# Far stretches of the attention visits in another order, and mixing weights loaded in quarters

## The chip, the cores and the metric

The kernel runs on one core of a Trainium2 chip. Its metric is the device time of one execution in microseconds, as the median of several runs. The engines are TensorE (PE, with its weight loads shown apart as PEld), VectorE (DVE), ScalarE (ACT), GpSimd (POOL) and SyncE (SP), which here only issues transfers.

## What is computed

The result is the sum of the input and two branches, which both read the same normalised input (2048 tokens of 512 features, bf16):

```python
xn = _layernorm(x)
return x + _A_ref(xn, A_wqkv, A_wo) + _B_ref(xn, B_w_in, B_w_sp, B_b_sp, B_w_out)

# A: attention, 32 heads of 16 features, sliding causal band of 256 keys
scores = einsum('bhqd,bhkd->bhqk', q, k) * Dh ** -0.5
mask = (idx[:, None] - idx[None, :] >= 0) & (idx[:, None] - idx[None, :] < 256)
p = softmax(where(mask, scores, -1e9)); o = einsum('bhqk,bhkd->bhqd', p, v)
A = o.reshape(B, S, D) @ wo

# B: gated unit that mixes along the tokens with a full 2048 x 2048 matrix
z = gelu(xn @ w_in); z1 = z[..., :688]; z2 = _layernorm(z[..., 688:])
g = einsum('ts,bsf->btf', w_sp, z2) + b_sp[None, :, None]
B = (z1 * g) @ w_out
```

## The kernel before

The 2048 tokens are 16 blocks of 128. The order of all work is written out by hand, as three strings of tokens (STAGE1, STAGE2, STAGE3). A token is a letter with arguments, and a table names the function that each letter calls; every engine gets its instructions in the order in which the tokens emit them. No planner moves anything, and each engine's queue is worked through in order.

Stage 1 loads and normalises the input (`a`, `A`, `b`), transposes it to feature-major `xnT` (by a DMA transpose on SP, token `d`, line 301, for 13 of the blocks; one such transpose is 128 x 512), and computes the gates: matmuls at line 311 (`z`), GELU on ACT (`y`). Its last tokens already project keys and queries (line 341), which are spread over the partitions by DMAs (`G` for keys, line 389; `F` for queries, line 368). For the first head group the spreads are issued on SP, for the others on POOL.

Stage 2 is the attention, in four groups of 8 heads, with the mixing and all projections woven between. For one head group the band of scores is laid out along one axis: key block kb owns 320 columns, the queries that its 128 keys can reach in two halves (its keys 64 to 127 are stored against queries shifted by 64, so that both half-blocks of keys share one layout). `S` computes 512 columns of scores for 4 heads (line 431, 8 to 16 matmuls in 32-row tiles), `X` takes the exponential on ACT (line 445), `M` multiplies the edges with a mask on DVE.

A **visit** (`V`, function `visit`, matmuls at line 512) multiplies these exponentials with the values. Unit u of a group is 256 queries. Visit i does two things at once: the *near* half of unit i, which reads keys 0 to 63 of each key block on partitions 0 to 63, and the *far* half of unit i - 1, which reads keys 64 to 127 on partitions 64 to 127. The two halves lie in different rows of the TensorE array and write different PSUM banks (`oP`), so they stream side by side. `av_half` lists a half's *stretches*: a stretch is one key block and one e (which four of the eight heads), n columns wide, and consists of four pairs of weight load and matmul, one for each of four heads, in four column strips of the array (64 rows x 17 columns of weights each). A half has up to eight stretches of 64, 128, 192 or 256 columns, 1280 columns in all for each strip; with u = 0 it has four of them, 768 columns near and 512 far. `av_half` yields each stretch with the column `at` which it begins, counted along its half, and `visit` sorts the stretches of both halves by that column, near before far where they are equal. This gives the order of the matmuls on TensorE. Before the change the far half runs from wide to narrow (256, 256, 192, 192, 128, 128, 64, 64), and the near half from narrow to wide, apart from that with u = 1, which runs from wide to narrow. There are 33 visits, i = 0 to 32, the last with a far half alone.

`N` normalises a finished unit on DVE. `H` is the mixing (line 553): 16 matmuls of 344 columns for each half of a block n. Its weights are a transposed 128 x 2048 slice of the mixing matrix, a tile of `wsp_pool`, which has three buffers. `load_wsp` (token `w`, line 545) fetches it with DMA transposes on SP, part 0 and part 1 in two tokens that stand next to each other. `w` of block n + 3 stands shortly behind the last mixing of block n, whose buffer it takes, and so it waits on SP until TensorE has read that buffer. `u` (line 566) transposes the gated result `z1u` of one block, also on SP. `O` and `R` are the output projections (lines 583 and 589), `v` stores a block of the result: blocks 0 to 2 on POOL, the others on SP (line 632). Stage 3 ends the projections.

SP therefore serves, in this order: input loads; transposes of x, with the weights of mixing block 0 (`w,0,0 w,0,1`) between the eighth and the ninth; the spreads of the first head group, with the weights of blocks 1 and 2 between them; then mixing weights and transposes of z1u in turn; at the end the stores.

Of the kernel before, what the change touches and what calls it, by code (L numbers as in the profile page):

```python
# [8 lines left out]
P = 128  # L9
# [12 lines left out]
NB = S_TOK // P  # L22
# [9 lines left out]
BAND = 320  # L32
WARM = 29
NCEN = 3


def kb_start(kb):
    return BAND * kb if kb < NB - 1 else BAND * (NB - 2) + 256


def kb_len(kb):
    return min(BAND, S_TOK - kb * P)
# [135 lines left out]
def kernel(  # L178
# [12 lines left out]
    nc = tc.nc  # L191
# [56 lines left out]
    xs = s1.tile([P, NB, D], BF, name="xs")  # L248
    xc = s1.tile([P, NCEN, D], BF, name="xc")
    xcT = s1.tile([P, NCEN, NDC, P], BF, name="xcT")  # L250

# [30 lines left out]
    def x_transpose(n, bank):  # L282
        xn = xc[:, n, :] if n < NCEN else xs[:, n, :]
        tp = banks[bank].bitcast(BF)[:, 0:512].rearrange("p (c q) -> p c q", c=NDC)
        for c in range(NDC):
            nc.tensor.transpose(out=tp[:, c, :], in_=xn[:, c * P : (c + 1) * P], identity=ident[:])  # L286

    def x_copy(n, bank, eng):
        tp = banks[bank].bitcast(BF)[:, 0:512].rearrange("p (c q) -> p c q", c=NDC)
        if n < NCEN:  # L290
            for c in (0, 2):
# [14 lines left out]
    def gate(n, half, tag, p0, p1):  # L306
        zp = zrot[tag]
        f0 = half * FH
        for c in range(2 * p0, 2 * p1):
            for lo, hi in Z_RANGES:  # L310
                nc.tensor.matmul(  # L311
                    zp[:, lo:hi],
                    lhsT=xcT[:, n, c, :] if n < NCEN else xnT[:, c, n * P : (n + 1) * P],
                    rhs=w_in_sb[:, c, f0 + lo : f0 + hi],
# [4 lines left out]
    def gelu(n, half, tag):  # L319
        zp = zrot[tag]  # L320
        dst = z1u[:, n + 1, 0:FH] if half == 0 else z2[:, n, :]

        scale = rstdx[:, n : n + 1] if n < NCEN else 1.0
        nc.scalar.activation(out=dst, in_=zp[:, 0:FH], func=ACT.Gelu_apprx_tanh, scale=scale)  # L324
# [142 lines left out]
    def av_half(G, u, half):  # L467

        a = 2 * u
        r0 = 64 * half
        bank = oP[(G * 8 + u) % 2]
        todo = []
        for kb in range(max(0, a - 2), a + 2):

            lo = max(0, a * P - kb * P - r0)
            hi = min(kb_len(kb) - (r0 if kb >= NB - 2 else 0), (a + 2) * P - kb * P - r0)
            assert lo < hi, (u, half, kb)
            todo += [(hi - lo, kb, lo, hi, e) for e in range(2)]  # L480

        up = half == 0 and (G * 8 + u) % 8 != 1
        todo.sort(key=lambda t: (t[0] if up else -t[0], t[1], t[4]))
        at = 0
        for i, (n, kb, lo, hi, e) in enumerate(todo):
            o0 = e * 256 + kb * P + lo + r0 - a * P
            col = (kb_start(kb) + lo) % RING
            yield at, [
                dict(
                    out=bank[32 * s : 32 * s + DH + 1, o0 : o0 + n],  # L490
                    lhsT=v_all[r0 : r0 + 64, kb, HG * G + 4 * e + s, :],
                    rhs=E[r0 : r0 + 64, 4 * e + s, col : col + n],
                    start=(half == 0 and i == 0),
                    stop=(half == 1 and i == len(todo) - 1),
                )
                for s in range(4)
            ]
            at += n

    def visit(i):  # L500

        top = list(av_half(i // 8, i % 8, 0)) if i < NG * 8 else []
        low = list(av_half((i - 1) // 8, (i - 1) % 8, 1)) if i >= 1 else []
        if not top:

            nc.tensor.matmul(
                oP[i % 2][0 : DH + 1, 0:1], lhsT=v_all[0:64, 0, 0, :], rhs=E[0:64, 0, 0:1],
                start=True, stop=True, skip_group_check=True,
            )
        for _, four in sorted(top + low, key=lambda t: t[0]):  # L510
            for args in four:
                nc.tensor.matmul(skip_group_check=True, **args)  # L512
# [26 lines left out]
    wsp_tiles = {}  # L539

    def load_wsp(n, part):
        if part == 0:
            wsp_tiles[n] = wsp_pool.tile([P, NB, P], BF, name="wspT")
        c0 = part * NB // 2
        nc.sync.dma_start_transpose(
            out=wsp_tiles[n][:, c0 : c0 + NB // 2, :],
            in_=B_w_sp[n * P : (n + 1) * P, c0 * P : (c0 + NB // 2) * P],
        )

    def mix(n, half, bank, c0, c1):  # L550
        w = wsp_tiles[n]
# [82 lines left out]
    def set_o():  # L634
# [7 lines left out]
        "Q": proj_q, "q": keep_q, "K": proj_k, "k": keep_k, "F": spread_q, "G": spread_k, "P": proj_v, "p": keep_v,  # L642
        "H": mix, "h": keep_mix, "u": transpose_u, "O": out_u, "R": out_o, "o": keep_out, "v": store_out,
        "w": load_wsp, "f": out_u_half, "g": out_o_half, "x": store_half, "r": load_xres, "m": set_o,
    }

# [68 lines left out]
    for r0 in (0, 64):  # L715
        nc.gpsimd.affine_select(
            out=mask[r0 : r0 + 64, 0, :], in_=mask[r0 : r0 + 64, 0, :], pattern=[[-1, 64]],
# [3 lines left out]
            out=mask[r0 : r0 + 64, 1, :], in_=mask[r0 : r0 + 64, 1, :], pattern=[[1, 64]],  # L721
# [54 lines left out]
```

## Time and profile before

| | |
|---|---|
| median of 3 runs | 258.38 us (258.15 to 258.97) |
| profiled execution, its own time | 258.61 us |
| its span, first to last instruction | 256.9 us |
| PE busy | 248.8 us (97%) |
| DVE busy | 186.2 us (72%) |
| ACT busy | 181.0 us (70%) |
| POOL busy | 92.0 us (36%) |
| granted TensorE clock | 1.000 |

A group row of the profile reads: line, engine, operation, written tile <- read tiles, rows * columns of the array, shapes, count | busy us, mean ns of one | idle us ahead of it, and what ended the idle time. A row of the timeline reads: start, duration, engine, line, operation, tiles, shape of the first of the merged instructions, count. SPq is SyncE's queue at work issuing a DMA; the time is that of the issue, not of the transfer. A row that names a line with three numbers (1232/1304/4387) gives the least, the median and the longest duration in ns. In the windows view a row is a stretch of time, its length, and for each engine the busy time and in brackets the number of instructions that touch it. The ends of matmuls are modelled by the profiler, so that a visit's length is read from the start of its first matmul to the start of the next work.

### The profile page before, as it was taken

What the parts mean: (1) busy time and instruction counts of PE and PEld (TensorE: products, weight loads), DVE (VectorE), ACT (ScalarE), POOL (GpSimd) and SP (SyncE); (2) the same over time, 40 slices, a digit from 0 to 9 for tenths busy, and PEclk for the clock granted to TensorE, in tenths of its full rate; (3) what the DMA queues carried; (4) which work ended last, traced back from release to release, by engine and by line L of the source; (5) the groups of instructions that cost most, each with busy time, mean ns of one, the idle gap of its engine ahead of it and who ended that gap; (6) DMA issues with size and microseconds to landing.
All of it is one profiled execution on the core that took longest, in us unless ns stands there. A gap on an engine that the chain in (4) does not pass through costs nothing.

```text
span 256.9 us, 9051 instructions
## 1 busy us (share of the span) xinstructions
PE 248.8 (97%) x3900; PEld 139.3 (54%) x3936; DVE 186.2 (72%) x412; ACT 181.0 (70%) x142; POOL 92.0 (36%) x172
## 2 busy tenths in 40 slices
PE   7999999999999999999999999999999999999995
PEld 6565555433456555655555655655555544444454
DVE  4887877888797676768775767758877487666764
ACT  3686566899978687777778776867687787777400
POOL 7514110430016176017288053603645343611110
PEclk9999999999999999999999999999999999999999
DMA  7985743269404886659969549998775632644432
GB/s 233 362 242 103 124 82 81 72 134 220 100 3 86 111 148 137 116 110 133 145 125 166 115 83 113 128 148 146 140 144 114 125 74 84 115 123 119 115 98 68
DMA packets 69945, 32.67 MB, mean 127 GB/s; under 512 B 60833, under 2 KB 66945, under 8 KB 69905
## 3 DMA queue, kind: packets, MB, share of 16 engines
q1 hardware_dynamic: 64000, 20.79, 44.1%
q0 software_dynamic: 4672, 9.97, 17.6%
q10 hardware_dynamic: 1232, 1.32, 1.5%
q8 instruction: 31, 0.51, 0.9%
q14 instruction: 10, 0.07, 0.1%
HBM read 8.41 MB, written 2.10 MB: 41 GB/s over the span
## 4 chain that ended last, share of the span: by engine, by line
PE 93%; ACT 3%; issue 1%; DMA 1%; DVE 1%
PE w L553 31%; PE sS L431 10%; PE w L341 10%; PE oP L512 8%; PE w L583 6%; PE zb L311 5%; PE za L311 5%; PE zo L311 5%; PE w L396 4%; PE w L589 4%; ACT E L445 2%; DMA xs<-in_A_x_dram 1%; PE w L286 1%; PE w L605 1%; PE tj L583 1%
## 5 line engine op out<-in xcount | busy, mean ns | idle before, releaser
L445 ACT ACTIVATE E<-sS 128x2048 bf16<-128x2048 f32 x76 | 142.6, 1877 | 41.9 <-PE sS L431 40.8
L553 PE MATMUL w<-z,wspT 128*128 128x344 bf16 x512 | 92.6, 310 | 0.7 <-issue 0.2
L553 PEld LDWEIGHTS <-wspT 128*128 128x128 bf16 x512 | 46.9, 98 | 31.5 <-issue 5.9
L389 POOL DMA_DIRECT2D kbd<-kz x48 | 29.5, 623 | 60.4 <-DVE kz L381 58.3
L368 POOL DMA_DIRECT2D q<-qs x54 | 28.0, 529 | 29.2 <-DVE qs L357 22.0
L454 DVE TENSOR_TENSOR E<-E,mask 128x1024 bf16<-128x1024 bf16 x52 | 34.7, 675 | 4.3 <-ACT E L445 4.3
L341 PE MATMUL w<-xnT,wqkv 128*128 128x512 bf16 x106 | 35.7, 380 | 0.7 <-issue 0.3
L431 PE MATMUL sS<-q,kbd 32*128 32x320 bf16 (+4 forms) x816 | 30.4, 244 | 0.3
L560 DVE SCALAR_TENSOR_TENSOR z1u<-w,b_all,z1u 128x344 bf16<-128x344 f32 x32 | 18.2, 568 | 16.4 <-PE w L553 16.3
L520 DVE STREAM_TRANSPOSE a<-oP 128x512 f32<-128x512 f32 x32 | 22.7, 709 | 5.4 <-PE oP L512 5.3
L512 PE MATMUL oP<-E,v_all 64*17 64x256 bf16 (+3 forms) x1920 | 24.8, 230 | 0.4 <-issue 0.4
L512 PEld LDWEIGHTS <-v_all 64*17 64x17 bf16 x1920 | 20.2, 85 | 9.0 <-issue 8.8
L311 PEld LDWEIGHTS <-xnT 128*128 128x128 bf16 x208 | 18.3, 98 | 12.4
L431 PEld LDWEIGHTS <-kbd 32*128 32x128 bf16 x816 | 12.2, 92 | 22.2 <-issue 20.0
L583 PE MATMUL w<-w_out_sb,z1u 128*128 128x512 bf16 x67 | 19.1, 380 | 0.5 <-issue 0.3
L577 POOL DMA_DIRECT2D wqkv<-in_A_x_dram x16 | 8.9, 558 | 28.3 <-DVE out_sb L597 27.5
L341 PEld LDWEIGHTS <-wqkv 128*128 128x128 bf16 x128 | 12.1, 98 | 9.6 <-issue 1.2
L329 DVE BATCH_NORM_STATS2 st<-z 128x6 f32<-128x344 bf16 x32 | 14.4, 492 | 2.6 <-ACT z L324 2.6
L396 PE MATMUL w<-wqkv,xnT 128*128 128x512 bf16 x63 | 16.2, 380 | 0.0
L533 DVE STREAM_TRANSPOSE oT<-b 128x256 bf16<-128x256 bf16 x32 | 14.2, 445 | 1.1
L381 DVE CAST kz<-w 128x256 bf16<-128x256 f32 x26 | 9.8, 418 | 6.5 <-PE w L341 4.4
L589 PE MATMUL w<-wo_sb,oT 128*128 128x512 bf16 x47 | 13.8, 380 | 0.0
(95 smaller groups left out, 248.9 us busy)
## 6 DMA issues: line engine op xcount, KB each, us to landing
kbd<-kz POOLq DMA_DIRECT2D x48, 64.0 KB, 3.3
q<-qs POOLq DMA_DIRECT2D x36, 64.0 KB, 3.8
wqkv<-in_A_x_dram POOLq DMA_DIRECT2D x16, 128.0 KB, 3.5
wqkv<-in_A_wqkv_dram SPq DMA_DIRECT2D x1, 1536.0 KB
out_dram<-out_sb SPq DMA_DIRECT2D x11, 128.0 KB, 2.7
xs<-in_A_x_dram SPq DMA_DIRECT2D x2, 512.0 KB, 7.5
kbd<-kz SPq DMA_DIRECT2D x16, 64.0 KB, 2.1
q<-qs SPq DMA_DIRECT2D x14, 64.0 KB, 2.3
```

The lines of the kernel that those rows point to most:

```text
L311: nc.tensor.matmul(zp[:, lo:hi], lhsT=xcT[:, n, c, :] if n < NCEN else xnT[:, c, n * P : (n + 1) * P], rhs=w_in_sb[:, c, f0 + lo : f0 + hi ...
L341: nc.tensor.matmul(banks[bank], lhsT=wqkv[:, c, col : col + P], rhs=xnT[:, c, tok : tok + 512], start=(c == 0), stop=(c == NDC - 1),)
L368: eng.dma_start(out=q2[h : P : 2, e, c : c + w], in_=t[64 * e : 64 * e + 64, src0 + at : src0 + at + w],)
L389: eng.dma_start(out=kbd[h : P : 2, slot : slot + 4, e, :], in_=t[64 * e : 64 * e + 64, h, :].rearrange("p (k m) -> p k m", k=4),)
L396: nc.tensor.matmul(banks[bank], lhsT=xnT[:, c, n * P : (n + 1) * P], rhs=wqkv[:, c, 2 * D : 3 * D], start=(c == 0), stop=(c == NDC - 1),)
L431: nc.tensor.matmul(s_bank(s)[:, off + o : off + o + w], lhsT=kbd[32 * s : 32 * s + 32, slot, ee, :], rhs=q2[32 * s : 32 * s + 32, ee, c : ...
L445: nc.scalar.activation(out=dst, in_=src, func=ACT.Exp, scale=SM_SCALE)
L454: nc.vector.tensor_tensor(out=reg, in0=reg, in1=mask[:].rearrange("p a m -> p (a m)").unsqueeze(1).to_broadcast([P, 8, 128]), op=ALU.mult,)
L512: nc.tensor.matmul(skip_group_check=True, **args)
L553: nc.tensor.matmul(banks[bank][:, 0:FQ], lhsT=w[:, c, :], rhs=z2[:, c, half * FQ : (half + 1) * FQ], start=(c == 0), stop=(c == NB - 1),)
L583: nc.tensor.matmul(banks[bank], lhsT=uT[:, c, :], rhs=w_out_sb[:, c, :], start=(c == 0), stop=False)
L589: nc.tensor.matmul(banks[bank], lhsT=oT[:, G, n * P : (n + 1) * P], rhs=wo_sb[:, G, :], start=False, stop=(G == NG - 1),)
```

## The change

Two edits are made.

First, in `av_half`, the stretches of a far half (half 1) with u > 0 are put in a fixed order after they have been sorted. `FAR` holds for u = 1 to 6 and gives widths of 192, 128, 128, 64, 192, 256, 256, 64 columns; `FAR_LAST` holds for u = 7 and gives 64, 128, 128, 256, 256, 192, 192, 64. With the sort in `visit`, this also changes how near and far stretches follow each other on TensorE. In the visits with u = 2 to 7 of the near half, whose changes lie at columns 64, 128, 256, 384, 576, 768 and 1024, the far half changed at 256, 512, 704, 896, 1024, 1152 and 1216; it now changes at 192, 320, 448, 512, 704, 960 and 1216. In the visits that begin a head group, the near half changes at 128, 256 and 512, and the far half now at 64, 192, 320, 576, 832, 1024 and 1216. Visits whose near half has u = 1 are as before.

Second, `load_wsp` issues two DMA transposes of 512 columns where it issued one of 1024, so that a tile comes in four transfers and not in two. Tokens and buffers are the same.

```diff
+FAR = (2, 4, 5, 6, 3, 0, 1, 7)
+FAR_LAST = (6, 4, 5, 0, 1, 2, 3, 7)
...
         todo.sort(key=lambda t: (t[0] if up else -t[0], t[1], t[4]))
+        if half == 1 and u:
+            todo = [todo[k] for k in (FAR_LAST if u == 7 else FAR)]
...
     def load_wsp(n, part):
         if part == 0:
             wsp_tiles[n] = wsp_pool.tile([P, NB, P], BF, name="wspT")
-        c0 = part * NB // 2
-        nc.sync.dma_start_transpose(
-            out=wsp_tiles[n][:, c0 : c0 + NB // 2, :],
-            in_=B_w_sp[n * P : (n + 1) * P, c0 * P : (c0 + NB // 2) * P],
-        )
+        for c0 in (part * NB // 2, part * NB // 2 + NB // 4):
+            nc.sync.dma_start_transpose(
+                out=wsp_tiles[n][:, c0 : c0 + NB // 4, :],
+                in_=B_w_sp[n * P : (n + 1) * P, c0 * P : (c0 + NB // 4) * P],
+            )
```

## The prediction

> **What bounds the kernel now.** I read the page's busy shares and chain first, then the waits of TensorE, then the timeline of its matmuls, and last the inside of one visit.
>
> ```profile
> PE 248.8 (97%) x3900; PEld 139.3 (54%) x3936; DVE 186.2 (72%) x412; ACT 181.0 (70%) x142; POOL 92.0 (36%) x172
> PE 93%; ACT 3%; issue 1%; DMA 1%; DVE 1%
> ...
> L445 ACT ACTIVATE E<-sS 128x2048 bf16<-128x2048 f32 x76 | 142.6, 1877 | 41.9 <-PE sS L431 40.8
> ```
>
> TensorE is busy for 97% of the span and makes 93% of the chain. The exponentials, the dearest group of another engine, idle 40.8 us waiting for TensorE's scores. So TensorE time saved or added inside the attention stage is kernel time.
>
> ```profile
> PEld L431 <- issue: 20.0, 58, 0.5
> PEld L512 <- issue: 8.8, 31, 0.6
> ...
> PEld L431 <- DMA kbd<-kz: 0.6, 2, 0.3
> PEld L431 <- DMA wo_sb<-in_A_wo_dram: 0.4, 1, 0.4
> PEld L431 <- DMA q<-qs: 0.3, 1, 0.3
> ```
>
> Nearly all of TensorE's gaps are "issue", 20.0/58 = 0.34 us each ahead of a group of scores. Only four gaps (1.3 us) are put down to a DMA, and at 0.3 to 0.4 us they are no longer than the issue gaps at the same place: TensorE does not wait for transfers. I therefore give the second part of the change no gain.
>
> ```profile
> 64.49 0.73 PE L512 MATMUL oP<-E,v_all 64*17 64x256 bf16 x48
> 65.15 1.04 PE L341 MATMUL w<-xnT,wqkv 128*128 128x512 bf16 x3
> ...
> 101.00 0.76 PE L512 MATMUL oP<-E,v_all 64*17 64x64 bf16 x64
> 101.68 0.40 PE L431 MATMUL sS<-q,kbd 32*128 32x128 bf16 x16
> ...
> 105.92 0.74 PE L512 MATMUL oP<-E,v_all 64*17 64x128 bf16 x48
> 106.62 0.41 PE L431 MATMUL sS<-q,kbd 32*128 32x64 bf16 x12
> ```
>
> These are three visits, each with the start of the next work behind it. In each the longer half streams 1280 columns. The visit with near u = 1 (far half: u = 0, 48 matmuls) takes 0.66 us, a usual one (64 matmuls) 0.68, one that begins a group (48) 0.70. So the order can win back about 0.02 to 0.04 us a visit, if 0.66 is the floor.
>
> The next view counts the visit at 101.00 from the inside. Each row is a window that begins ahead of it, so the (x) say how many matmuls and how many weight loads have started by the window's end.
>
> ```profile
> 100.95:101.02 0.07, 0.03 (x8) 0.03 (x8) 1.00 1.05 223
> 100.95:101.10 0.15, 0.10 (x16) 0.11 (x24) 1.00 1.07 220
> 100.95:101.20 0.25, 0.20 (x28) 0.21 (x33) 1.00 1.10 225
> 100.95:101.23 0.28, 0.23 (x28) 0.24 (x34) 1.00 1.09 222
> 100.95:101.25 0.30, 0.26 (x32) 0.26 (x37) 1.00 1.08 220
> 100.95:101.31 0.36, 0.32 (x36) 0.32 (x37) 1.00 1.09 222
> 100.95:101.40 0.45, 0.41 (x45) 0.41 (x48) 1.00 1.09 219
> 100.95:101.50 0.55, 0.51 (x56) 0.51 (x60) 1.00 1.09 220
> 100.95:101.60 0.65, 0.60 (x64) 0.61 (x64) 1.00 1.09 215
> ...
> L512 PE MATMUL oP<-E,v_all 64*17 64x256 bf16 x480 | 21.9, 271 | 0.4 <-issue 0.4
> L512 PE MATMUL oP<-E,v_all 64*17 64x64 bf16 x480 | 14.1, 191 | 0.0
> ```
>
> Up to 33 loads go as fast as matmuls make room (24 by 0.10). Then the loads stop twice: the 34th comes only at about 0.23, and after the 37th nothing goes between 0.25 and 0.31. From then on they go evenly, 12 in 0.10 us (48 to 60), 8.3 ns a pair, to the end. My reading: 32 pairs of load and matmul are at hand when the visit begins; each later pair is let in when the matmul 32 places ahead of it is complete, in order. The two durations give the column's price, (271 - 191)/192 = 0.42 ns. Matmuls 1 to 4 are the near half's 64-column stretch, 5 to 8 the far half's first, of 256 columns, which start by 0.02. If pair 33 is let in about 0.23 after matmul 1, then 192 more columns (0.08) and 0.01 of later start put pair 37, which waits for matmul 5, at 0.32: the second stop ends there. So the visit's loss is not made where the halves change together (near and far both at column 256, and both at 1024) but by this shortage of pairs.
>
> **Part 1, the order of the far stretches.** No matmul, load, column or wait is added or removed. In the usual visit (far u = 1 to 6, four groups: 24 visits) the far half goes from 256, 256, 192, 192, 128, 128, 64, 64 columns to 192, 128, 128, 64, 192, 256, 256, 64. Step by step, from the start of the visit:
>
> 1. Which pairs are late. Before, pairs 37 to 40 are the far half's second 192. After, they are again the far half's second 192, since nine stretches (four far, five near) start ahead of it.
> 2. When they are let in. Before: 0.32. After, matmul 5 has 192 columns, not 256: 64 x 0.42 ns = 0.027 earlier, 0.293. The fourth pair of the stretch comes 3 x 8.3 ns = 0.025 later: 0.345 before, 0.318 after.
> 3. What that column strip still has to stream. Before: 192 + 128 + 128 + 64 + 64 = 576 columns = 0.240, done at 0.585 (the table: all 64 matmuls started by 0.60, the last of 64 columns). After: 192 + 256 + 256 + 64 = 768 columns = 0.320, done at 0.638.
> 4. The near half. Its second 192 was pairs 33 to 36, let in from 0.23. After, the changes come so thick at the beginning that it is pairs 41 to 44: 0.293 + 4 x 0.0083 = 0.326, the fourth 0.351, and 192 + 256 + 256 = 704 columns = 0.293 are left: 0.644.
>
> The visit's streams end at 0.64 instead of 0.585: +0.055 us, 24 times, +1.3 us. The change moves far-half changes to the front, where the pairs run out, and leaves the long stretches for after the shortage. Nothing hides it: TensorE's next work starts when the visit has drained.
>
> The visits that begin groups 2, 3 and 4 get the other order (64, 128, 128, 256, 256, 192, 192, 64). There pairs 33 to 36 become the second 256, freed by matmul 1 (a near 128): 0.23 + 0.027 = 0.255, fourth 0.28, and 256 + 192 + 192 + 64 = 704 columns are left, 0.293: 0.573. The row at 105.92 gives 0.70; less the 0.095 between 0.585 and the 0.68 of the usual visit it streamed for about 0.60. I take 0 for these three (bounds: -0.04 each, the floor of 0.66, to +0.02). The last visit (32 matmuls, far half alone) has all its pairs at hand: 0. Bounds of the part: from -0.02 x 24 - 0.04 x 3 = -0.6 us (all at 0.66), through 0, to +1.5 us (0.06 each). I take +1.3, since the rows inside the visit show the two stops.
>
> The Trainium skill, page "TensorE: Matmul & The Clock Gate", section "Part 3: Packing small matmuls — row/col tiling", has a rule that speaks for the change: a weight load overlaps matmuls in flight only where its row group is another one. By it, two halves that change at the same column could not hide their loads, and keeping the changes apart would bring all visits to 0.66, 257.8 us in all, against my 259.7. The count above does not bear it out: by 0.10 there are 24 loads for 16 matmuls, four loads ahead in each row group while that row group streams.
>
> **Part 2, the mixing weights in quarters.** Each of 16 tiles takes four DMA issues on SP where it took two. No byte more is moved.
>
> ```profile
> L545 SPq DMA_TRANSPOSE wspT<-in_B_w_sp_dram x32: 1232/1304/4387, 25.8 to 183.6; - x32
> ...
> L301 SPq DMA_TRANSPOSE xnT<-xs x5: 1191/1258/1897, 29.4 to 35.4; - x5
> DMA to landing us min/median/max: 2.5/2.5/3.8
> ...
> 25.84 2.66 SPq L545 DMA_TRANSPOSE wspT<-in_B_w_sp_dram  x2
> 29.38 7.19 SPq L301 DMA_TRANSPOSE xnT<-xs  x5
> 38.47 5.38 SPq L389 DMA_DIRECT2D kbd<-kz  x8
> ...
> 63.01 2.58 SPq L389 DMA_DIRECT2D kbd<-kz  x4
> 66.98 2.40 SPq L368 DMA_DIRECT2D q<-qs  x4
> ...
> 185.01 22.19 SPq L566 DMA_TRANSPOSE z1u<-z1u  x6
> 219.93 0.37 SPq L632 DMA_DIRECT2D out_dram<-out_sb  x1
> ...
> 34.43 1.33 PE L311 MATMUL zb<-w_in_sb,xnT 128*128 128x512 bf16 x8
> ...
> 78.86 0.40 PE L431 MATMUL sS<-q,kbd 32*128 32x128 bf16 x12
> ```
>
> The transposes of x have a quarter's size, 128 x 512, and cost SP 1.26 us each against 1.30 for a half: the issue is a fixed price. With the 0.04 between issues a tile takes 5.2 us of SP instead of 2.66, +2.5. What stands behind it on SP:
>
> - Tile 0, at 25.84, ahead of five transposes of x. They start at 31.05 instead of 29.38. Landing at the median 2.5 later makes 33.55, at the longest, 3.8, it makes 34.85; the first reader (gate of block 13) starts at 34.43. So 0 to +0.4 us, and I take 0, the median. The five end at 37.5, ahead of the key spread that starts at 38.47.
> - Tiles 1 and 2 delay the spreads of the first head group by 2.5 and then 5.1 us. SP idles from 65.6 to 66.98, so the last spread of queries goes at 70.7, ends at 73.1 and lands by about 76 (2.5 as above); its first reader is the score group at 78.86. Cover 3 us: 0.
> - Tiles 3 to 15 wait for the tile three before to be read out and are wanted two tiles of mixing later. Behind them come the transposes of z1u; the last six end at 207.2 and SP then idles until 219.93, and their readers, the output projections of blocks 7 to 12, come after that store, which is of block 3: 0.
> - The mix now waits at four of its sixteen loads and not at two, for data that has landed: 0. Smaller transposes also let other packets through earlier, but TensorE waits for none: 0 (above).
>
> Part 2: 0, bounds 0 to +0.4.
>
> **The sum.** The profiled execution took 258.61 us (span 256.9): 258.6 + 1.3 = 259.9. The median of the runs is 0.2 lower, so I say 259.7. About 0.3%, 0.8 us, is what a measurement of this kernel can tell from no change.
>
> **The rivals.**
>
> A. The changes that meet are what costs. Place: columns 256 and 1024 of 24 usual visits. Price: 0.02 to 0.03 us each, so that all visits come to 0.66: 258.4 - 0.6 = 257.8, up to -0.8 with the group beginnings. For it: visits without a meeting inside take 0.66. Against: those have only 48 pairs, and the loads stop at pairs 34 and 38, not at a meeting. It decides where pair 37 is held by something other than matmul 5. Chance 0.13, about half of it beyond 0.3%.
>
> B. The shortage is there but the streams make it up, or the pairs are let in per half and not in one order: visits of 0.67 to 0.70, 258.2 to 259.0. For it: one visit was read in full. Against: the even 8.3 ns after 0.31 shows one common supply. Chance 0.17.
>
> C. My visits and a stall of the gates in stage 1: 259.7 + 0.4 = 260.1. For it: the margin is 0.9 us at the median and negative at the longest landing. Chance 0.13.
>
> My forecast: 0.57. Slower: 0.57 + 0.13 = 0.70. Within 0.3%: 0.17 and 0.05 of A, 0.22. Faster: 0.08. The range runs from B's low end, 258.2, to C's 260.1 and the +1.5 with it, 260.6, and leaves out A and the outer ends, 0.2. My forecast's own range is 259.3 to 260.1.
>
> **What would show it.** Usual visits should take 0.73 to 0.74 from start to next work, their 38th load coming near 0.29 and their last matmul starting near 0.61. Visits with u = 1 stay at 0.66 and group beginnings at 0.68 to 0.70. If usual visits take 0.66, A holds and the reading of the two stops is wrong. In stage 1 the gate of block 13 should follow the matmul before it without a gap; a gap there is C. SP should hold 64 issues of the mixing weights of about 1.25 us, and the score group that was at 78.86 should come only the visits' delay later.

## The result and the profile after

The changed kernel takes 259.74 us in the median of 6 runs (259.48 to 259.94); the kernel before, beside it, 258.34 us (258.15 to 258.97, 6 runs). The ratio is 1.0051, with a 95% interval of 1.0038 to 1.0064: slower by half a per cent, 1.4 us. The profiled execution took 259.94 us against 258.61. In the changed kernel the line numbers move: visits are line 518 (512 before), scores 435 (431), gates 315 (311), mixing 559 (553), transposes of x 305 (301), loads of the mixing weights 551 (545).

The page of the changed kernel, span, busy time and chain by engine:

```profile
span 258.2 us, 9121 instructions
...
PE 252.4 (98%) x3936; PEld 138.1 (53%) x3936; DVE 186.5 (72%) x412; ACT 181.1 (70%) x142; POOL 92.0 (36%) x172
...
PE 93%; ACT 3%; DMA 2%; DVE 1%; issue 0%; ACTq 0%
```

The bound is the same, TensorE with 93% of the chain. DMA has grown from 1% to 2%, issue has shrunk from 1% to 0%. PE's busy time is no measure of the difference, since the trace of before lacks 36 matmul records (3900 of 3936).

The three kinds of visit, in the timeline of TensorE's matmuls (start, duration, instructions), each with the next work behind it:

```profile
65.14 0.73 PE L518 MATMUL oP<-E,v_all 64*17 64x256 bf16 x48
65.81 1.04 PE L345 MATMUL w<-xnT,wqkv 128*128 128x512 bf16 x4
...
101.92 0.81 PE L518 MATMUL oP<-E,v_all 64*17 64x64 bf16 x64
102.66 0.40 PE L435 MATMUL sS<-q,kbd 32*128 32x128 bf16 x16
...
106.90 0.74 PE L518 MATMUL oP<-E,v_all 64*17 64x128 bf16 x48
107.60 0.41 PE L435 MATMUL sS<-q,kbd 32*128 32x64 bf16 x12
```

The usual visit now takes 102.66 - 101.92 = 0.74 us, not 0.68; the others take what they took, 0.67 (0.66 before) and 0.70. Over all undisturbed usual visits of the two traces the means are 0.743 and 0.688, a difference of 0.055.

The visit at 101.92 from the inside. Each window begins 0.05 ahead of the visit; (x) counts the matmuls and the weight loads that have started by its end:

```profile
101.87:102.12 0.25, 0.20 (x32) 0.20 (x33) 1.00 0.00 0
101.87:102.15 0.28, 0.23 (x33) 0.23 (x34) 1.00 0.00 0
101.87:102.20 0.33, 0.28 (x36) 0.28 (x37) 1.00 0.00 0
101.87:102.22 0.35, 0.30 (x38) 0.30 (x38) 1.00 0.00 0
101.87:102.42 0.55, 0.50 (x55) 0.50 (x62) 1.00 0.00 0
101.87:102.52 0.65, 0.60 (x62) 0.60 (x64) 1.00 0.00 0
101.87:102.55 0.68, 0.63 (x64) 0.60 (x64) 1.00 0.00 0
```

The two stops of the loads are still there, at 33 and at 37. The second ends between 0.28 and 0.30, where it ended after 0.32 before, so the pairs come earlier, and yet the last matmul starts only between 0.60 and 0.63. By 0.50 nearly all loads are done, 62 against 60, but only 55 matmuls have started where it was 56: what is left is streaming, not loading.

SP's queue and TensorE in stage 1, timelines of the changed kernel:

```profile
26.26 6.23 SPq L551 DMA_TRANSPOSE wspT<-in_B_w_sp_dram  x4
32.59 6.46 SPq L305 DMA_TRANSPOSE xnT<-xs  x5
...
35.08 1.34 PE L315 MATMUL zb<-w_in_sb,xnT 128*128 128x512 bf16 x8 [0.69 <-DMA xnT<-xs]
```

The gate of block 13 now waits 0.69 us for its transpose. It starts at 35.08 and not at 34.43, in an execution whose projections of stage 1 began 0.21 earlier (25.27 against 25.48): a delay of 0.86 us.

What adds up in the two profiled executions, to the start of the last visit (248.50 before, 249.80 after, +1.30): the earlier begin -0.21, stage 1 +0.86, the visits +1.10 (below), and a remainder of -0.45. Behind the remainder stands something new: a pause of 0.7 us inside a visit near 125 us, in the trace of before, is not there in the trace after. Before, the timeline shows that visit in two pieces:

```profile
124.36 0.74 PE L512 MATMUL oP<-E,v_all 64*17 64x64 bf16 x50
125.51 0.30 PE L512 MATMUL oP<-E,v_all 64*17 64x256 bf16 x14 [0.41 <-issue]
```

After it stands undivided at 125.40 and the next work follows at 126.14. Some of the 0.7 us is lost again in later waits, so that -0.45 is what is left of it at the last visit.

### The profile page after: what moved, and what is told of

Its sections match the earlier page's. It is cut to its first block, busy times and chain, and to the rows that moved or that the text cites. A ratio compares the mean times of both kernels' runs of the same rounds, so it can differ in the third digit from the quotient of the medians.

```text
span 258.2 us, 9121 instructions
## 1 busy us (share of the span) xinstructions
PE 252.4 (98%) x3936; PEld 138.1 (53%) x3936; DVE 186.5 (72%) x412; ACT 181.1 (70%) x142; POOL 92.0 (36%) x172
## 4 chain that ended last, share of the span: by engine, by line
PE 93%; ACT 3%; DMA 2%; DVE 1%; issue 0%; ACTq 0%
PE w L559 30%; PE w L345 11%; PE sS L435 10%; PE oP L518 8%; PE w L589 6%; PE w L400 5%; PE zb L315 5%; PE za L315 5%; PE w L595 4%; PE zo L315 4%; ACT E L449 2%; DMA xs<-in_A_x_dram 1%; DMA xnT<-xs 1%; PE w L290 1%; PE ti L589 1%; PE w L611 1%
## 5 line engine op out<-in xcount | busy, mean ns | idle before, releaser
L345 PE MATMUL w<-xnT,wqkv 128*128 128x512 bf16 x128 | 41.1, 380 | 0.0
L518 PE MATMUL oP<-E,v_all 64*17 64x128 bf16 (+3 forms) x1920 | 25.8, 230 | 0.0
L518 PEld LDWEIGHTS <-v_all 64*17 64x17 bf16 x1920 | 19.3, 85 | 8.3 <-issue 8.1
```

Of the source, the lines that this page charges most:

```text
L345: nc.tensor.matmul(banks[bank], lhsT=wqkv[:, c, col : col + P], rhs=xnT[:, c, tok : tok + 512], start=(c == 0), stop=(c == NDC - 1),)
```

## The experiments

Each kernel is compared with runs of the kernel before on the same chip. The table gives the usual visit (mean from start to next work, from the trace), the pause near 125 us (the longest time without the start of a weight load in that visit), the time from the first weight load of stage 1's projections to the start of the last visit, and the ratio of the timed runs.

| kernel | visit us | pause us | projection to last visit us | ratio (95%) |
|---|---|---|---|---|
| before | 0.688 | 0.73 | 223.02 | 1 |
| changed | 0.743 | none | 224.52 | 1.0051 (1.0038 to 1.0064) |
| changed, again | 0.743 | none | 224.14 | 1.0034 (1.0020 to 1.0049) |
| order alone | 0.743 | 0.51 | 224.08 | 1.0045 (1.0031 to 1.0060) |
| quarters alone | 0.688 | none | 222.78 | 0.9997 (0.9985 to 1.0010) |
| apart, wide first | 0.674 | none | 222.61 | 1.0004 (0.9991 to 1.0018) |
| meeting, wide first | 0.674 | 0.34 | 222.51 | 1.0003 (0.9989 to 1.0017) |
| narrow second | 0.776 | none | 224.31 | 1.0056 (1.0034 to 1.0078) |
| changed, block 0 in halves | 0.744 | none | 223.57 | 1.0047 (1.0030 to 1.0063) |
| quarters for block 0 alone | 0.69 | 0.57 | 223.64 | 1.0004 (0.9982 to 1.0026) |
| quarters but for block 0 | 0.69 | none | 222.53 | 1.0007 (0.9987 to 1.0028) |
| meeting, wide first, quarters but for block 0 | 0.674 | none | 222.37 | 1.0001 (0.9985 to 1.0017) |

Three things must be kept in mind with it. From trace to trace the first projection begins up to 1.1 us earlier or later (25.27 to 26.39), and the intervals of the ratios reach 0.3 to 0.6 us to either side, so that effects of a few tenths of a us are seen in the traces and not in the ratios.

The column of the pause is about one visit only. The visit near 178 us has a pause of the same kind in three traces: 0.25 us in the order alone, 0.65 in the changed kernel traced again, 0.84 with quarters for block 0 alone. In the second of them:

```profile
177.89 0.77 PE L518 MATMUL oP<-E,v_all 64*17 64x64 bf16 x55
178.99 0.29 PE L518 MATMUL oP<-E,v_all 64*17 64x256 bf16 x9 [0.33 <-issue]
```

And the end of the program is not equally long in all kernels. From the start of the last visit to the end of the span it takes 8.39 to 8.42 us in eight traces, but 8.98 to 8.99 in the three kernels that load block 0 in halves and the others in quarters, and 8.76 with quarters for block 0 alone. The last matmul and the last work of VectorE end 5.4 and 5.9 us after that visit's start in all twelve; the difference lies in the closing waits of SP's queue. DRAIN rows are instructions with which the program closes on that queue; here in the kernel before and with quarters but for block 0 (last visit at 248.50 and 247.80):

```profile
L771 SPq DRAIN  x3: 7/7/7, 256.1 to 256.4; - x3
...
L772 SPq DRAIN  x3: 7/7/130, 255.5 to 256.3; - x3
```

The last of the three starts 7.9 us after the last visit in the first, 8.5 in the second. Why the closing waits differ was not tested.

### The order alone

```diff
         todo.sort(key=lambda t: (t[0] if up else -t[0], t[1], t[4]))
+        if half == 1 and u:
+            todo = [todo[k] for k in ((6, 4, 5, 0, 1, 2, 3, 7) if u == 7
+                                      else (2, 4, 5, 6, 3, 0, 1, 7))]
```

> The new order of the far stretches alone, with the mixing weights in halves as before. Shortage of pairs (my theory): usual visits 0.74 us from start to next work, +0.055 each on 24 visits, 1.2 to 1.3 us over the kernel before, about 259.6; the gate of block 13 without a gap ahead of it. If the whole change is slower by stage 1 alone (the rival that the visits do not matter in the sum), within 0.3 us of the kernel before.

Measured: 259.67 us against 258.62, ratio 1.0045 (1.0031 to 1.0060). The timeline of TensorE:

```profile
101.10 0.81 PE L514 MATMUL oP<-E,v_all 64*17 64x64 bf16 x64
101.84 0.40 PE L431 MATMUL sS<-q,kbd 32*128 32x128 bf16 x16
```

The visit takes 0.74 as in the changed kernel, there is no gap in stage 1, and nearly the whole loss is there. This trace also prices the visits without the change's other effects: from the first projection to the last visit it takes 224.08 - 223.02 = 1.06 us longer; the pause near 125 is 0.21 shorter, and the one near 178, of 0.17 beyond the usual visit, is new: 1.06 + 0.21 - 0.17 = 1.10 us for 24 visits.

### The quarters alone

```diff
-        c0 = part * NB // 2
...
-            out=wsp_tiles[n][:, c0 : c0 + NB // 2, :],
...
+        for c0 in (part * NB // 2, part * NB // 2 + NB // 4):
...
+                out=wsp_tiles[n][:, c0 : c0 + NB // 4, :],
```

> The quarters alone, with the old order. If SP's longer issue delays the transposes of x: a gap of 0.8 to 0.9 us ahead of the gate of block 13, as in the changed kernel, and usual visits at 0.69. Time by that: +0.9 us, less what the quarters win back near 125 us (0.5 us in the comparison of the two traces), so +0.3 to +0.9. If the quarters cost nothing, as my prediction took it: within 0.3 us of the kernel before.

Measured: 258.57 us against 258.62, ratio 0.9997 (0.9985 to 1.0010). The visit is the old one. SP and TensorE in stage 1, timeline:

```profile
25.78 6.15 SPq L545 DMA_TRANSPOSE wspT<-in_B_w_sp_dram  x4
32.02 6.46 SPq L301 DMA_TRANSPOSE xnT<-xs  x5
...
34.52 1.34 PE L311 MATMUL zb<-w_in_sb,xnT 128*128 128x512 bf16 x8
```

SP is as late as in the changed kernel, but the gate of block 13 is held up by only 0.09 us. The timed runs put the second part of the change at nothing, within 0.4 us.

### Apart or meeting, with a wide stretch early

Two orders tell the shortage of pairs from the meeting of changes. In the first the far half goes 192, 256, 256, 192, 64, 128, 128, 64 columns, and none of its changes falls on one of the near half. In the second it goes 128, 256, 256, 192, 192, 128, 64, 64, and three of them do. Both keep the old order for u = 7 and load in halves.

```diff
+        if half == 1 and u:
+            todo = [todo[k] for k in ((0, 1, 2, 3, 4, 5, 6, 7) if u == 7
+                                      else (2, 0, 1, 3, 6, 4, 5, 7))]  # the first
+                                      else (4, 0, 1, 2, 3, 5, 6, 7))]  # the second
```

> Halves as before; far stretches of u = 1 to 6 as 192, 256, 256, 192, 64, 128, 128, 64 columns, so that again no change of the far half meets one of the near half, but the wide ones stand early. u = 7 as before. If changes that meet were the cost and the given order had another fault: like any order without a meeting. Shortage of pairs: few changes fall early, the late pairs have little left to stream, visits of 0.67 us (25 ns below 0.69 at most), 24 times, 0.3 to 0.5 us faster than before.

> Halves as before; far stretches of u = 1 to 6 as 128, 256, 256, 192, 192, 128, 64, 64 columns: three changes meet one of the near half (columns 128, 384, 1024), where two did before. u = 7 as before. If meetings cost: usual visits longer than 0.69 us, by 0.01 to 0.015. Shortage of pairs: the first far stretch is complete 128 columns (0.053 us) sooner, so the 38th load comes near 0.27 and not 0.32, and visits take 0.67 us, 0.3 to 0.5 us faster than before in all.

Measured: 258.69 us, ratio 1.0004 (0.9991 to 1.0018), and 258.64 us, ratio 1.0003 (0.9989 to 1.0017). One visit in the timeline of the first:

```profile
101.85 0.74 PE L514 MATMUL oP<-E,v_all 64*17 64x64 bf16 x64
102.52 0.40 PE L431 MATMUL sS<-q,kbd 32*128 32x128 bf16 x16
```

and of the second:

```profile
101.40 0.74 PE L514 MATMUL oP<-E,v_all 64*17 64x64 bf16 x64
102.07 0.40 PE L431 MATMUL sS<-q,kbd 32*128 32x128 bf16 x16
```

Without a meeting the visit takes 0.743 (changed) or 0.674 (first), with three of them 0.674 (second). Meetings decide nothing, and the rival A falls. What the two have in common is that the long stretches lie early, so that little is left to stream behind the shortage. The gain of 0.014 a visit, 0.3 us in all, for which 0.3 to 0.5 us had been expected in the time, is beyond what the timed runs can tell.

### A narrow stretch second

The far half goes 256, 64, 128, 64, 128, 256, 192, 192: only one change meets, and the late pairs have the most columns behind them.

```diff
+        if half == 1 and u:
+            todo = [todo[k] for k in ((0, 1, 2, 3, 4, 5, 6, 7) if u == 7
+                                      else (0, 6, 4, 7, 5, 1, 2, 3))]
```

> Halves as before; far stretches of u = 1 to 6 as 256, 64, 128, 64, 128, 256, 192, 192 columns: one change meets one of the near half (column 256), where two did before. If meetings cost: usual visits a little shorter than 0.69 us, time as before or faster. Shortage of pairs: the changes come thickest right behind the first wide stretch and 640 columns are left when the late pairs arrive, visits of about 0.77 to 0.78 us, +0.085 each, about +2.0 us in all, slower than the changed kernel.

Measured: 260.36 us against 258.80, ratio 1.0056 (1.0034 to 1.0078). The timeline:

```profile
101.24 0.84 PE L514 MATMUL oP<-E,v_all 64*17 64x64 bf16 x64
102.01 0.40 PE L431 MATMUL sS<-q,kbd 32*128 32x128 bf16 x16
```

The visit came out as worked out, 0.776 over all. In the time it makes 1.5 us (0.9 to 2.0), and 24 x 0.088 is 2.1, just outside: as with the order alone, not all of the visits' loss seems to reach the end.

The visits can now be compared from the inside. These windows begin 0.05 ahead of the visit; first this kernel, whose far half begins with 256 columns, then the one with three meetings, which begins with 128:

```profile
101.19:101.55 0.36, 0.31 (x36) 0.32 (x37) 1.00 1.09 223
101.19:101.56 0.37, 0.32 (x38) 0.33 (x38) 1.00 1.09 221
```

```profile
101.35:101.66 0.31, 0.26 (x33) 0.26 (x37) 1.00 1.09 219
101.35:101.67 0.32, 0.27 (x36) 0.27 (x38) 1.00 1.10 222
```

The 38th load has come by 0.32 with 256 columns first, by 0.30 with 192 (the changed kernel, above) and by 0.27 with 128: 0.02 to 0.03 for each 64 columns, which take 0.027 to stream (64 x 0.42 ns). This is what follows if pair 37 is let in when matmul 5, the first of the far half, is through.

### Block 0 in halves, and in quarters alone

The changed kernel with the tile of block 0 loaded in two transfers, and the kernel before with only that tile in four:

```diff
+        step = NB // 2 if n == 0 else NB // 4   # changed, block 0 in halves
+        step = NB // 4 if n == 0 else NB // 2   # quarters for block 0 alone
+        for c0 in range(part * NB // 2, (part + 1) * NB // 2, step):
+            nc.sync.dma_start_transpose(
+                out=wsp_tiles[n][:, c0 : c0 + step, :],
+                in_=B_w_sp[n * P : (n + 1) * P, c0 * P : (c0 + step) * P],
+            )
```

> The changed kernel with the weights of mixing block 0 in halves again, all others in quarters. If the gap in stage 1 comes from block 0's two more issues on SP: the first of the five transposes of x behind them goes out near 29.4 and not near 32.6, no gap ahead of the gate of block 13, usual visits still 0.74, and a time 0.1 to 0.9 us below the changed kernel's on the same chip. If the gap has another source: the gap stays.

> The kernel before with block 0's weights alone in quarters, old order of the far stretches. If block 0 is the source: its last quarter takes 2.2 to 2.3 us to issue, the transposes of x go out near 32 and not 29.4, a gap of 0.1 to 0.9 us ahead of the gate of block 13, and the same on the time over the kernel before. If not: as the kernel before.

Measured: 260.36 us against 258.80, ratio 1.0047 (1.0030 to 1.0063); and 259.19 us, ratio 1.0004 (0.9982 to 1.0026). Neither bears out a stall of stage 1 in the timed runs. With block 0 in halves the time should have come out 0.1 to 0.9 us below the changed kernel's on the same chip (259.60, next experiment), and it came out above it, though the intervals of the two ratios overlap. Its trace does gain 0.95 us up to the last visit (223.57 against 224.52), but 0.57 of that goes at the end of the program. SP's queue with block 0 in halves:

```profile
26.31 2.66 SPq L552 DMA_TRANSPOSE wspT<-in_B_w_sp_dram  x2
30.18 7.32 SPq L305 DMA_TRANSPOSE xnT<-xs  x5
```

and in the second, with four transfers, TensorE below:

```profile
26.44 5.19 SPq L546 DMA_TRANSPOSE wspT<-in_B_w_sp_dram  x4
31.73 7.32 SPq L301 DMA_TRANSPOSE xnT<-xs  x5
...
35.35 1.33 PE L311 MATMUL zb<-w_in_sb,xnT 128*128 128x512 bf16 x8
```

With quarters the transposes of x begin 1.5 us later, but the gate of block 13 follows without a gap. Later transposes alone make no delay: the gate's turn comes 8.95 us after the first projection in each of the ten traces without a gap, and here the first of the five transposes landed 8.67 after it. In the changed kernel it landed 9.75 after it, and that is the whole gap.

### The changed kernel again

> The changed kernel once more, as the measure for the other three on this chip and as a second profile. Usual visits 0.74 us again; the gap ahead of the gate of block 13 anywhere from 0.1 to 0.9 us, since it follows from when block 0's last quarter is issued; +1.2 to +1.6 us over the kernel before.

Measured, on the same chip as the three before: 259.60 us against 258.80, ratio 1.0034 (1.0020 to 1.0049). SP and TensorE in stage 1:

```profile
25.58 5.20 SPq L551 DMA_TRANSPOSE wspT<-in_B_w_sp_dram  x4
30.88 7.11 SPq L305 DMA_TRANSPOSE xnT<-xs  x5
...
34.43 1.33 PE L315 MATMUL zb<-w_in_sb,xnT 128*128 128x512 bf16 x8
```

The same program had no gap here. The four issues took 5.20 us, as priced, against 6.23 in the first profile of the changed kernel, and the transposes began at 30.88 against 32.59. Of the four traces with block 0 in quarters, the last quarter took 2.2 to 2.3 us to issue in two (the changed kernel and the quarters alone), and those two are the ones with a delay (0.86 and 0.09). In the other two the lengthened issue is the first transpose of x (2.1 and 1.9 us), and before it was the second (1.9). In the changed kernel the lengthened one overlaps a 16 KB transfer of the instruction queue at 30.09 that takes 1.34 us. Over the twelve traces, 115 of the 120 DMA transposes whose issue took more than 1.6 us overlap such a transfer of 16 KB, but only 118 of the 800 shorter ones do. Which of the two holds up the other was not tested.

### Quarters for the later tiles, in the old order and in the best one

In six of the six traces with later tiles in quarters the pause near 125 us is missing, counting these two; with halves it is there in four of six. (The pause near 178 us stands in one of the six with quarters and in two of the six with halves.) If it cost 0.5 us in the runs too, the following should beat the kernel before. The first is the order with three meetings (0.674 a visit), the second the old order, both with block 0 in halves and all others in quarters.

```diff
+        step = NB // 2 if n == 0 else NB // 4
+        for c0 in range(part * NB // 2, (part + 1) * NB // 2, step):
```

> What the runs so far point to: far stretches of u = 1 to 6 as 128, 256, 256, 192, 192, 128, 64, 64 columns (visits of 0.674 us in the trace of that order, -0.014 each, 24 times, -0.3 us), block 0's weights in halves (no gap in stage 1) and all other weights in quarters (no pause inside the visit near 125 us, which cost 0.3 to 0.7 us in four of the six traces with halves there). Sum if all of it counts in the timed runs: -0.5 to -0.8 us, 0.2 to 0.3% faster than before. If the pause and the gap are only chances of single executions: -0.3 us, within 0.3%.

> The old order, block 0's weights in halves, all others in quarters. If quarters there remove the pause near 125 us: the 51st load of that visit without a pause, the 16 KB instruction transfer ahead of it before 122 us, and up to 0.5 us faster than before. If the pause does not depend on them: as the kernel before, within 0.3%.

Measured: 258.69 us against 258.53, ratio 1.0001 (0.9985 to 1.0017), and 258.83 us, ratio 1.0007 (0.9987 to 1.0028). Neither is faster. In the trace both do what was expected of them: the visit of the pause, in the second,

```profile
124.14 0.76 PE L512 MATMUL oP<-E,v_all 64*17 64x64 bf16 x64
```

is whole, and from the first projection to the last visit they take 222.37 and 222.53 us, 0.65 and 0.49 less than before. But in both kernels the end of the program takes 8.98 us against 8.39, so that 0.59 of the 0.65 is lost again in the first, and all of the 0.49 in the second. That is enough for ratios of 1.000 to 1.001, as far as one trace of each can say; how often the pause occurs in the timed runs stays open. (The profiled execution of the first took 259.44 us because its projections also began 0.8 us later.) No order and no division of the transfers that was run beats the kernel before.

## Why the prediction came out right, point by point

**The bound.** TensorE still makes 93% of the chain, and the runs follow the visits' length: at or under the old one the ratio is 1.000 to 1.001, with 0.743 it is 1.003 to 1.005, with 0.776 it is 1.006.

**The pairs at hand.** The reading of the two stops holds. In the steps of part 1: the second stop was to end at 0.293 (it ended between 0.28 and 0.30), the last matmul to start near 0.61 (between 0.60 and 0.63), the visit to take 0.055 more (0.055). The same sums gave the visit with a narrow second stretch, and the 38th load moves with the width of the far half's first stretch. (So TensorE's queue is not worked through strictly in order, as was said of every engine: its weight loads run ahead of its matmuls, 62 against 55 by 0.50 in the changed visit.) Rival A falls: without any meeting the visits took 0.743 or 0.674, not 0.66, and three meetings cost nothing. Rival B falls with the visit's 0.743. The rule that stood beside A (the Trainium skill, page "TensorE: Matmul & The Clock Gate", section "Part 3: Packing small matmuls — row/col tiling": a weight load overlaps matmuls in flight only where its row group is another one) is not borne out by these traces, in which three meetings left the visit at 0.674.

**The other visits.** Group beginnings were put at 0 with bounds of -0.04 to +0.02. They took 0.700, 0.695 and 0.674 us after, 0.700, 0.694 and 0.674 before.

**The sum of the visits.** The step "24 times, +1.3 us" is mis-sized: 1.1 us arrive. (The timed runs, 1.0 to 1.7 us for the whole change, cannot tell the two apart.) The step that failed is "Nothing hides it: TensorE's next work starts when the visit has drained". Behind some visits stand scores that wait for an exponential to free their bank, and there the longer visit only shortens the wait. Such a visit in the changed kernel's timeline, with its next work:

```profile
73.80 0.81 PE L518 MATMUL oP<-E,v_all 64*17 64x64 bf16 x64
74.65 0.40 PE L435 MATMUL sS<-q,kbd 32*128 32x320 bf16 x8
...
192.89 0.81 PE L518 MATMUL oP<-E,v_all 64*17 64x64 bf16 x64
193.63 0.40 PE L435 MATMUL sS<-q,kbd 32*128 32x320 bf16 x8
```

and the same two before:

```profile
73.14 0.76 PE L512 MATMUL oP<-E,v_all 64*17 64x64 bf16 x64
73.99 0.40 PE L431 MATMUL sS<-q,kbd 32*128 32x320 bf16 x8
...
191.92 0.76 PE L512 MATMUL oP<-E,v_all 64*17 64x64 bf16 x64
192.66 0.40 PE L431 MATMUL sS<-q,kbd 32*128 32x320 bf16 x8
```

From start to next work both take the same in both kernels, 0.85 and 0.74. The exponential on ScalarE that the first of them waits for, in the changed kernel, ends at 72.72 + 1.88 = 74.60, and the scores follow at 74.65:

```profile
72.72 1.88 ACT L449 ACTIVATE E<-sS 128x2048 bf16<-128x2048 f32 x1
```

The 1.1 is what the trace of the order alone gives, 0.2 less than 24 x 0.055; these two visits are 0.11 of that. Four further visits, near 78, 146, 215 and 234 us, pass on 0.02 to 0.05 instead of 0.055, together 0.07 less; the rest was not traced to its places.

**SP in stage 1.** Part 2 was taken at 0, with bounds of 0 to +0.4; the runs of the quarters alone give 0 (-0.4 to +0.3 us), but the changed kernel's profile had +0.86, beyond the bound. The step that failed is the price of "5.2 us of SP instead of 2.66", made of four median issues. The group of the mixing weights, of the changed kernel:

```profile
L551 SPq DMA_TRANSPOSE wspT<-in_B_w_sp_dram x64: 1188/1266/2531, 26.3 to 187.1; - x64
...
DMA to landing us min/median/max: 2.6/3.8/5.8
```

The median, 1266 ns, is what was said; but one issue in this stretch can take 1 us more. The row of five transposes shown in the prediction says so in its longest, 1897 ns, and the sum didn't use it. With it the bound would have been +1.0 and rival C dearer. The longer issue is 1.0 of the 1.75 us by which the transposes came later than reckoned, counted from the first projection (7.32 us after it, not 5.57). Most of the rest is that SP came to the tile 0.99 us after the first projection, not 0.36; in the eleven other traces it is 0.04 to 0.59.

**The rest of SP.** The score group that was at 78.86 is at 79.57, 0.71 later: no more than stage 1's delay and the visits, less the earlier begin, make by then. No transfer of the later tiles is waited for.

**"TensorE does not wait for transfers … no gain".** This is the step that the traces put in doubt. One gap of 0.7 us, which the view of waits counts as issue, is missing in all six traces with quarters, though one of them has the like in another visit (0.65 us near 178). The timed runs show no gain, so the 0 stands as a number. The reason given for it, that TensorE waits for no transfer since nearly all its gaps are called issue, is not shown.

**The total.** 259.7 was forecast and 259.74 measured. In the profiled execution that closeness is partly luck: +0.86 of stage 1 is mostly made up by -0.45 of the pause and -0.21 of the begin. In the runs it is the mechanism: the order alone gives 1.0045, the whole change 1.0051 and, measured again, 1.0034.

## What to carry to other kernels

Where many small matmuls with their own weights stream in parallel strips, count loads and matmuls from the start of the burst: if the loads stop at a fixed number of pairs, it is the order of widths that sets the end. Let the stretches that hold those places be finished early, and put long stretches ahead of the stop and narrow ones behind it; where the changes fall against those of the other half didn't matter. When a queue's work is doubled ahead of a deadline, price it with the longest issue of the profile beside the median, and look at more than one trace before a gap in it is called the change's. Compare begin, middle and end of the span apart: a gain in the middle can be lost in the end.

## What was not expected of the hardware

- **The burst's supply of pairs.** The 38th load comes by 0.27, 0.30 and 0.32 us for a first far stretch of 128, 192 and 256 columns, as it would if pair 37 were let in when matmul 5 is through; then pairs come every 8.3 ns. That this is so regular as to price a visit to 0.01 us was more than hoped for.
- **Issue of a DMA transpose on SP.** It costs 1.27 us for 512 columns (median of 64) and 1.30 for 1024. Single ones in stage 1 took 1.9 to 2.3 us in the traces shown, and nearly all long ones overlap a transfer of the instruction queue.
- **The pauses inside visits.** Near 125 us it is always the same load, the 51st of that visit. In the four traces that have it, it goes 1.3 to 1.4 us after the end of a 16 KB transfer of the instruction queue (124.19, load at 125.51, in the kernel before); in the eight others that transfer ends earlier against the visit, and the load goes at its due time. Near 178 us it is the 57th load, 1.3 to 1.5 us after such a transfer in the three traces that have it. The view of waits calls it issue. The transfer ahead of the visit near 125 ends 1.7 to 2.7 us before that visit in the six traces with later tiles in quarters, and 0.2 to 1.4 us before it in the six with halves; ahead of the visit near 178 there is no such difference. This is a correlation in twelve traces; what the load waits for, and whether the smaller transposes are what lets the transfer end sooner, was not tested.
- **The end of the program.** From the start of the last visit it takes 8.39 to 8.42 us in eight traces and 8.76 to 8.99 in four, with the same work of TensorE and VectorE in it; the difference lies in the closing waits of SP.
